# Cosine attention and a leaky-ReLU layer: the seventh pair turned by DMA, the 11th pair's norm behind the visit's first step, the last slot's scores and totals ahead of most early first products

## The chip, the cores and the metric

The kernel runs on one core of one Trainium2 chip. The metric is device time in microseconds (us). Its engines are TensorE (PE; PEld is its weight load), VectorE (DVE), ScalarE (ACT), GpSimd (POOL) and SyncE (SP). Each runs its own instructions in order and waits on semaphores for the others. SP, ACT and POOL also issue DMAs.

## The reference

```python
def _attn_ref(q, k, v, tau):                 # 8 batches, 12 heads, 448 rows, 64 columns
    q_n = q / (np.linalg.norm(q, axis=-1, keepdims=True) + 1e-06)
    k_n = k / (np.linalg.norm(k, axis=-1, keepdims=True) + 1e-06)
    scores = np.matmul(q_n, k_n.transpose(0, 1, 3, 2)) / tau
    scores = scores - np.max(scores, axis=-1, keepdims=True)
    attn = np.exp(scores)
    attn = attn / (np.sum(attn, axis=-1, keepdims=True) + 1e-09)
    return np.matmul(attn, v).astype(np.float32)

def _moe_ref(x, w_in, w_out):                # x: 3584 x 768; w_in: 768 x 2048; w_out: 2048 x 768
    h = x @ w_in
    g = np.maximum(0.01 * h, h)
    return (g @ w_out).astype(np.float32)
```

The attention's output, heads side by side, is the x of the second function.

## The kernel before

The program order is written out by hand: each engine carries out its instructions in the order in which the Python code emits them, so the place of a call in the code is its place in every queue that it uses.

**Pairs.** Two heads of one batch form a pair `s`, six to a batch, 48 in all, counted from 0: the seventh pair is `s` = 6, the first of batch 1, and the 11th is `s` = 10. A pair goes through these steps:

- its q and k are loaded (`load_pairs`, `load_qk`) into one of six places of `raw_sb`;
- `squares` (usually on POOL), `sums` (DVE) and `roots` (two small ACT instructions) give the norms;
- `normalise` (DVE: two small instructions and two large ones, L222) writes the normalised pair into a `qn` tile. The pool of these has three buffers, so pair `s` is written where pair `s` - 3 lay, and waits until that one has been read;
- `transposes` turns it, into a `qkT` tile: seven TensorE instructions (`one`, L236) into a PSUM bank and one copy (DVE up to pair 7, ACT after it), or, from pair 10 on (`DMA_FROM`), one DMA that SP issues (L254);
- `scores` (`key_tiles`) multiplies keys by queries (L280) in tiles of two PSUM banks, three for each pair and one for the remainders of two pairs, and ACT takes the exponentials (L292).

**Slots.** Two pairs form a slot `j`, three to a batch (`NQ`). `totals` sums the exponentials on TensorE, `reciprocals` inverts the sums on ACT (L339, L340), `products` multiplies by v on TensorE (L320), and `scale` writes the result into `xT` on DVE (L361). `attend` does this for one slot, `attend_two` for two.

**Chunks.** The 3584 rows are taken in eight chunks `c` of 384 and 512 rows in turn. The first products (`first`, L384) multiply a chunk's `xT` by `w_in`, six inner steps for each of 16 blocks `m`, and ACT writes hT. The second products (`groups`, L459) multiply hT by `w_out`.

**Order.** First come the six pairs of batch 0, with the scores of pair 5 last. Between these stand first products of chunk 0 that need the first two slots alone (`begin`: inner steps 0 to 3 of blocks 0 to 3). Then `attend(2)` does the last slot of batch 0, with the rest of those early products behind its value products. Then `firsts(0, ...)` does chunk 0's 16 blocks. Its table `between` says what is emitted ahead of which block: norms, sums and transposes of pairs 6 to 11 and loads of v. Then comes the visit of chunk 0 (`visit`): its second products, with the scores of batch 1 (pairs 6 to 11) dealt out between them after given numbers of steps (`wide`). Its table `norms` says what is emitted after which step. `attend_batch(1)` follows, then `firsts(1, ...)`, and so on for the other chunks.

**Holding GpSimd.** `hold` is a one-element POOL copy of a given tile: what POOL does next stays behind it. `norm(s)` emits `roots`, `normalise` and (unless told not to) `transposes`; then, by pair, loads of later pairs on SP, a `hold` on pair `s` and the squares of a later pair on POOL. The weights `w_out` are loaded by POOL's queue behind a `hold` on `xT`, ahead of `norm(7)`.

Of the kernel before, what the change touches and what calls it, by code (L numbers as in the profile page):

```python
# [16 lines left out]
def kernel(  # L17
# [19 lines left out]
    NPAIR = H // 2  # L37
    NSLOT = B * NPAIR
    NQ = NPAIR // 2
# [115 lines left out]
    def load_v(j):  # L155
        if j >= B * NQ:
            return
        b, jj = divmod(j, NQ)
        vb[j] = vbp.tile([128, 4, 3, D], BF16, name="v_b")
        gp.dma_start(out=vb[j], in_=main(v, b, 4 * jj, 4))  # L160
# [12 lines left out]
    def squares(s, engs=(gp, gp)):  # L173
        if s >= NSLOT:
            return
        tiles = []
        for x, eng, name in zip(raw[s], engs, ("sq0", "sq1")):
            sq = sqp.tile(list(x.shape), F32, name=name)
            if eng is nc.scalar:
                nc.scalar.activation(sq, x, func=AF.Square)  # L180
            else:
                eng.tensor_tensor(sq, x, x, op=ALU.mult)  # L182
            tiles.append(sq)
        sqs[s] = tiles

    def sums(s, parts=(0, 1)):
        if s >= NSLOT:
            return
        if s not in ss:
            ss[s] = smp.tile([128, 14], F32, name="ss")  # L190
        for i in parts:
            o = ss[s][:, 0:8] if i == 0 else ss[s][:, 8:14]
            nc.vector.tensor_reduce(  # L193
                o.rearrange("p (h t) -> p h t", h=2), sqs[s][i], axis=AX.X, op=ALU.add
            )

    def roots(s):
        if s >= NSLOT:
            return
        nc.scalar.activation(ss[s], ss[s], func=AF.Ln, bias=tiny)  # L200
        nc.scalar.activation(ss[s], ss[s], func=AF.Exp, scale=0.5)  # L201
# [11 lines left out]
    def normalise(s):  # L213
        if s >= NSLOT:
            return
        r = smp.tile([128, 14], F32, name="r")
        nc.vector.tensor_scalar_add(ss[s], ss[s], 1e-6)  # L217
        nc.vector.reciprocal(r, ss[s])
        qn[s] = qnp.tile([128, 7, 2, D], BF16, name="qn")
        for x, lo, hi, r0 in ((raw[s][0], 0, 4, 0), (raw[s][1], 4, 7, 8)):  # L220
            nt = hi - lo
            scalings[s] = nc.vector.tensor_tensor(  # L222
                qn[s][:, lo:hi],
                x.rearrange("p h t d -> p t h d"),
                r[:, r0 : r0 + 2 * nt].rearrange("p (h t) -> p t h", h=2)
                .unsqueeze(3).to_broadcast([128, nt, 2, D]),
                op=ALU.mult,
            )
# [19 lines left out]
    def transposes(s):  # L248
        if s >= NSLOT:
            return  # L250
        dst = qtp.tile([128, 7, 128], BF16, name="qkT")
        qkT[s] = dst.rearrange("p t c -> p (t c)")
        if s >= DMA_FROM:
            nc.sync.dma_start(  # L254
                out=dst, in_=qn[s].rearrange("p t h d -> p (t h d)"), transpose=True
            )
            return
        tp = transposed()
        one(tp, s, 0, 7)
        copy = nc.scalar.copy if s > 7 else nc.vector.tensor_copy  # L260
        copy(out=dst, in_=tp)  # L261
# [3 lines left out]
    def scores(s, kis):  # L265
        key_tiles([(s, ki) for ki in kis])
# [108 lines left out]
    def first(c, m, kts=range(KT)):  # L375

        c0, n = chunk_cols(c)
        if c not in hT:
            hT[c] = htp.tile([128, MT, 512], BF16, name="hT")
        if (c, m) not in pms:  # L380
            pms[c, m] = banks(1)
        pm = pms[c, m]
        for kt in kts:
            nc.tensor.matmul(  # L384
                out=pm[:, :n],
                lhsT=w_in_sb[:, kt, m * 128 : (m + 1) * 128],
                rhs=xT[c // 2][:, kt, c0 : c0 + n],
                start=(kt == 0), stop=(kt == KT - 1),
            )
        if kts[-1] == KT - 1:  # L390
            nc.scalar.activation(  # L391
                out=hT[c][:, m, :n], in_=pms.pop((c, m))[:, :n], func=AF.Prelu, alpha=0.01
            )
            if (c, m, 0) in kept:
                given_back((c, m, 0))
# [116 lines left out]
    def hold(x):  # L512
        seen = smp.tile([128, 1], F32, name="seen")
        gp.tensor_copy(out=seen, in_=x)  # L514
# [122 lines left out]
    def begin(m, kts):  # L637

        if (0, m) not in pms:
            pms[0, m] = banks(1, (0, m, 0))  # L640
        first(0, m, kts)

    scores(5, (0, 1))
    products(1, 1)
    for m in range(2):
        begin(m, range(2))
    for e in range(2):
        scale(1, e)
    scores(5, (2,))
    for m in range(2):  # L650
        begin(m, range(2, KT - 2))
    scores(5, (3,))
    for m in range(2, SOON):
        pms[0, m] = banks(1, (0, m, 0))
    begin(2, range(KT - 2))
    sums(6)
    sums(7)
    roots(6)

    def attend(j, behind=()):  # L660
        totals(j)
        reciprocals(j)
        po = banks(2)
        for e in range(2):
            products(j, e, po[:, e])
        for fn in behind:
            fn()
        for e in range(2):
            scale(j, e)
# [30 lines left out]
    def norm(s, transposed=True):  # L700
        if s >= NSLOT:
            return
        roots(s)
        normalise(s)
        if transposed:
            transposes(s)
        if s == 10:
            return
        for x in (12, 13) if s == 11 else (s + 4,) if s > 11 else ():
            load_qk(x)  # L710
        hold(qn[s][:, 6, 0, 0:1])
        if s == 11:
            squares(12)
        if s != 9:
            squares(s + (3 if s < 9 else 2))

    def firsts(b, begun, between):

# [25 lines left out]
    def at(*steps):  # L744
# [5 lines left out]
    four_late = (at(5, 11, 16, 16, 24),) * 3 + (at(6, 16, 16),)  # L750

    deals["apart"] = False
    attend(NQ - 1, [lambda m=m: first(0, m, range(KT - 2)) for m in range(3, SOON)])
    normalise(6)
    hold(xT[0][:, 2 * NQ - 2, 0:1])
    load_w_out(range(0, MT, MT // 4))
    norm(7, False)
# [2 lines left out]
    firsts(  # L760
        0, SOON, {
            4: [lambda: norm(8, False)],
            5: [lambda: transposes(6)],
            6: [lambda: sums(9)],
            8: [lambda: transposes(7)],
            9: [lambda: norm(9, False)],
            10: [lambda: transposes(8)],
            11: [lambda: sums(10), lambda: load_v(3)],
            12: [lambda: norm(10), lambda: load_v(4)],
            13: [lambda: transposes(9), lambda: load_v(5), lambda: load_v_rem(1)],  # L770
            15: [lambda: sums(11)],
        },
# [2 lines left out]
    for b in range(B):  # L775
        tokens = chunk_cols(b)[1] // 128
        if b == B - 1:
            for ts in range(tokens):
                for half in range(2):
                    second(b, ts, half)  # L780
            break
        order = [[((ts, 0), (ts, 1))] for ts in range(tokens)]
        if b == 0:
            order = [order[0] + order[1], order[2]]
        norms = {(0, 18): [lambda: norm(11)]}
        if b:
            norms = {}
            for i in range(tokens - 1 + (b == 1)):
                norms[i, 4 if tokens > 3 else 12] = [lambda s=ready: norm(s)]
                ready += 1  # L790
                norms[i, 20] = [lambda s=ready: sums(s)]
        else:
            ready += 2
        visit(
            b, order, norms,
            wide if b == 0 else four_late if b == 1 else three if tokens == 3 else four,
        )
        attend_batch(b + 1)
        for j in range((b + 2) * NQ, (b + 3) * NQ):
            load_v(j)  # L800
        load_v_rem(b + 2)
        s = ready
        between = {0: [lambda s=s: norm(s)], 1: [lambda s=s: sums(s + 1)]}
        if b == 0:
            between = {
                0: [lambda: sums(13)], 1: [lambda: norm(13), lambda: sums(14)],
                4: [lambda: norm(14), lambda: sums(15)], 7: [lambda: norm(15)],
                9: [lambda: sums(16)], 11: [lambda: norm(16)], 14: [lambda: sums(17)],
            }
            ready += 5  # L810
        elif tokens == 3:
            between.update({
                4: [lambda s=s: norm(s + 1), lambda s=s: sums(s + 2)],
                7: [lambda s=s: norm(s + 2), lambda s=s: sums(s + 3)],
                10: [lambda s=s: norm(s + 3)], 13: [lambda s=s: sums(s + 4)],
            })
            ready += 4
        else:
            between.update({
                4: [lambda s=s: norm(s + 1)], 5: [lambda s=s: sums(s + 2)],  # L820
                8: [lambda s=s: norm(s + 2)], 12: [lambda s=s: sums(s + 3)],
            })
            ready += 3
        firsts(b + 1, 0, between)
# [35 lines left out]
```

## Time and profile before

| what | value |
|---|---|
| median of 3 runs | 407.03 us (406.74 to 407.2) |
| profiled execution, device time | 407.09 us |
| its span, first to last instruction | 405.3 us |
| granted TensorE clock, mean | 1.000 |
| ACT busy | 265.0 us (65%) |
| DVE busy | 187.7 us (46%) |
| POOL busy | 140.7 us (35%) |
| share of the chain on PE | 93% |
| mean DMA traffic | 134 GB/s |

The stages that the change lies in, from the chain of waits: early products and the last slot of batch 0, 28.7 to 35.8 us; the rest of chunk 0's first products, to 50.35; the visit of chunk 0, to 69.97; the attention of batch 1, to 76.85.

How to read the lines that follow. A line of the chain of waits is start, length and what ran; a timeline line is start, length, engine, line of the code, operation, tiles written and read. "L384" is line 384 of the code. Queue q0 is POOL's DMA queue, q1 is SP's and ACT's. A window line gives busy time and number of instructions for PE, PEld, DVE, ACT and POOL, then the granted clock, the DMA share and GB/s.

### The profile page before, as it was taken

What the parts mean: (1) busy time and instruction counts of PE and PEld (TensorE: products, weight loads), DVE (VectorE), ACT (ScalarE), POOL (GpSimd) and SP (SyncE); (2) the same over time, 40 slices, a digit from 0 to 9 for tenths busy, and PEclk for the clock granted to TensorE, in tenths of its full rate; (3) what the DMA queues carried; (4) which work ended last, traced back from release to release, by engine and by line L of the source; (5) the groups of instructions that cost most, each with busy time, mean ns of one, the idle gap of its engine ahead of it and who ended that gap; (6) DMA issues with size and microseconds to landing.
All of it is one profiled execution on the core that took longest, in us unless ns stands there. A gap on an engine that the chain in (4) does not pass through costs nothing.

```text
span 405.3 us, 10173 instructions
## 1 busy us (share of the span) xinstructions
PE 398.5 (98%) x4096; PEld 225.0 (56%) x4096; DVE 187.7 (46%) x403; ACT 265.0 (65%) x458; POOL 140.7 (35%) x215
## 2 busy tenths in 40 slices
PE   8999999999999999999999999999999999999996
PEld 3335655544555655544886555544687555544564
DVE  6987912684665624454452626256361731130021
ACT  5996799556874689654876569745786559844300
POOL 4995823363344513343141513255122500000000
PEclk9999999999999999999999999999999999999999
DMA  7999999697689826576486844686477721110033
GB/s 190 252 227 246 214 184 212 180 182 180 147 195 154 153 60 175 118 126 174 73 185 142 131 113 118 160 117 152 68 177 125 96 45 40 40 41 2 0 78 79
DMA packets 100735, 54.21 MB, mean 134 GB/s; under 512 B 69424, under 2 KB 95440, under 8 KB 100688
## 3 DMA queue, kind: packets, MB, share of 16 engines
q1 hardware_dynamic: 76400, 40.13, 42.0%
q0 software_dynamic: 23440, 12.92, 23.2%
q8 instruction: 32, 0.52, 0.5%
q10 hardware_dynamic: 848, 0.52, 0.4%
q14 instruction: 15, 0.12, 0.1%
HBM read 45.61 MB, written 11.01 MB: 140 GB/s over the span
## 4 chain that ended last, share of the span: by engine, by line
PE 93%; POOL 3%; DVE 1%; DMA 1%; issue 1%; ACT 0%; POOLq 0%
PE ps L384 36%; PE ps L459 31%; PE ps L320 11%; PE ps L280 8%; PE ps L421 5%; POOL sq L182 1%; PE ps L307 1%; DMA raw_sb<-in_k_dram 1%; POOL v_rem L167 1%; DVE qn L222 1%; PE ps L236 1%; POOL raw_sb L132 0%; POOL v_b L160 0%; POOL seen L514 0%; DVE qkT L261 0%
## 5 line engine op out<-in xcount | busy, mean ns | idle before, releaser
L384 PE MATMUL ps<-xT,w_in_sb 128*128 128x384 bf16 (+1 forms) x768 | 148.0, 353 | 0.0
L459 PE MATMUL ps<-w_out_sb,hT 64*128 64x384 bf16 x1536 | 144.0, 323 | 0.0
L292 ACT ACTIVATE pe<-ps 128x896 bf16<-128x896 f32 x144 | 124.5, 917 | 17.2 <-PE ps L280 15.3
L384 PEld LDWEIGHTS <-w_in_sb 128*128 128x128 bf16 x768 | 74.0, 98 | 71.7 <-issue 4.0
L391 ACT ACTIVATE hT<-ps 128x384 bf16<-128x384 f32 (+1 forms) x128 | 67.2, 544 | 66.6 <-PE ps L384 66.1
L459 PEld LDWEIGHTS <-hT 64*128 64x128 bf16 x1536 | 84.4, 94 | 44.8 <-PE ps L459 4.2
L182 POOL TENSOR_TENSOR sq<-raw_sb 128x512 f32<-128x512 f32 x90 | 82.4, 937 | 12.5 <-DMA raw_sb<-in_k_dram 11.9
L222 DVE TENSOR_TENSOR qn<-raw_sb,r 128x512 bf16<-128x512 f32 x96 | 56.6, 631 | 2.0 <-DMA raw_sb<-in_q_dram 0.3
L280 PE MATMUL ps<-qkT 64*128 64x448 bf16 (+1 forms) x384 | 54.8, 353 | 1.1 <-DVE qkT L261 0.6
L193 DVE TENSOR_REDUCE ss<-sq 128x6 f32<-128x384 f32 (+1 forms) x95 | 54.3, 610 | 1.1 <-POOL sq L182 1.0
L471 DVE COPY osb<-ps 128x384 f32<-128x384 f32 x41 | 21.2, 553 | 69.7 <-PE ps L459 38.8
L514 POOL CAST seen<-qn 128x1 f32<-128x1 bf16 x46 | 9.1, 198 | 124.3 <-DVE qn L222 124.0
L217 DVE TENSOR_SCALAR ss<-ss 128x14 f32<-128x14 f32 x48 | 10.2, 213 | 75.7 <-ACT ss L201 75.6
L361 DVE TENSOR_TENSOR xT<-ps,rb 128x448 bf16<-128x448 f32 x48 | 27.8, 620 | 24.6 <-ACT rb L340 24.4
L160 POOL DMA_DIRECT2D v_b<-in_v_dram x24 | 18.6, 776 | 39.6 <-PE ps L320 39.6
L320 PE MATMUL ps<-pe,v_b 128*32 128x448 bf16 x576 | 32.0, 353 | 0.0
L280 PEld LDWEIGHTS <-qkT 64*128 64x128 bf16 (+1 forms) x384 | 17.7, 97 | 17.6 <-issue 7.3
L339 ACT ACTIVATE rb<-ps 128x448 f32<-128x448 f32 x24 | 12.9, 538 | 14.9 <-PE ps L320 13.9
L320 PEld LDWEIGHTS <-v_b 128*32 128x32 bf16 x576 | 15.1, 97 | 12.0 <-issue 0.6
L427 DVE COPY osb<-ps 128x384 f32<-128x384 f32 (+1 forms) x9 | 4.6, 513 | 36.6 <-PE ps L421 36.6
L421 PE MATMUL ps<-w_out_sb,hT 128*128 128x384 bf16 (+1 forms) x144 | 21.0, 308 | 0.0
L292 ACT ACTIVATE pr<-ps 128x896 bf16<-128x896 f32 x24 | 20.7, 924 | 0.2 <-PE ps L280 0.2
(52 smaller groups left out, 188.2 us busy)
## 6 DMA issues: line engine op xcount, KB each, us to landing
raw_sb<-in_q_dram SPq DMA_DIRECT2D x46, 192.0 KB, 3.2
raw_sb<-in_k_dram SPq DMA_DIRECT2D x44, 192.0 KB, 3.2
out_dram<-osb SPq DMA_DIRECT2D x30, 192.0 KB, 3.0
v_b<-in_v_dram POOLq DMA_DIRECT2D x24, 192.0 KB, 4.9
out_dram<-osb SPq DMA_DIRECT2D x12, 384.0 KB, 2.6
w_out_sb<-in_moe_w_out_dram POOLq DMA_DIRECT2D x4, 768.0 KB, 15.8
w_in_sb<-in_moe_w_in_dram POOLq DMA_DIRECT2D x3, 512.0 KB, 8.4
w_in_sb<-in_moe_w_in_dram POOLq DMA_DIRECT2D x2, 768.0 KB, 12.7
```

The source lines that it names most:

```text
L182: eng.tensor_tensor(sq, x, x, op=ALU.mult)
L193: nc.vector.tensor_reduce(o.rearrange("p (h t) -> p h t", h=2), sqs[s][i], axis=AX.X, op=ALU.add)
L222: scalings[s] = nc.vector.tensor_tensor(qn[s][:, lo:hi], x.rearrange("p h t d -> p t h d"), r[:, r0 : r0 + 2 * nt].rearrange("p (h t) -> p ...
L280: nc.tensor.matmul(out=out[:, a, :S], lhsT=x[rows, c0:c1], rhs=x[rows, 0:S], start=True, stop=True,)
L292: nc.scalar.activation(out=dst, in_=sc[:, :, :S], func=AF.Exp, scale=inv_tau)
L320: nc.tensor.matmul(out=x[32 * g : 32 * g + 32, :S], lhsT=weights(g, ki) if ki < 3 else rem(g), rhs=pe[s][:, ki, a, :] if ki < 3 else pr[j] ...
L361: scalings[j, e] = nc.vector.tensor_tensor(xT[m][:, 2 * jj + e, half * S : (half + 1) * S], pos.pop((j, e))[:, :S], rbs[j], op=ALU.mult,)
L384: nc.tensor.matmul(out=pm[:, :n], lhsT=w_in_sb[:, kt, m * 128 : (m + 1) * 128], rhs=xT[c // 2][:, kt, c0 : c0 + n], start=(kt == 0), stop= ...
L391: nc.scalar.activation(out=hT[c][:, m, :n], in_=pms.pop((c, m))[:, :n], func=AF.Prelu, alpha=0.01)
L421: nc.tensor.matmul(out=po2[:, :n], lhsT=hT[c][:, m, ts * 128 : (ts + 1) * 128], rhs=w_out_sb[:, m, lo : lo + n], start=(m == 0), stop=(m = ...
L459: done[p][i] = nc.tensor.matmul(out=pos2[p][:, i, :HALF], lhsT=hT[c][rows, m, ts * 128 : (ts + 1) * 128], rhs=w_out_sb[rows, m, half * HAL ...
L471: copy(out=osb[c, ts][:, half * HALF : (half + 1) * HALF], in_=po2[:, i, :HALF])
```

## The change

- `transposes` turns pair 6 by DMA too.
- `norm`, `normalise` and `transposes` of pair 6 stand together right behind `attend(2)`; its roots move from ahead of `attend(2)` to there, its transposes from block 5 of `firsts(0, ...)`.
- Of the early first products, two of block 1 move behind the third score tile of pair 5, two of block 1 behind its remainder tile, and two of block 2 behind the value products of `attend(2)`.
- The squares of pairs 10 and 11, until now behind the norms of pairs 7 and 8, both stand behind pair 9's, under one `hold`. The norms of pairs 7 and 8 hold POOL no longer.
- The sums of pair 10 move from block 11 to block 12, and its norm from block 12 to the visit, after the first step.

```diff
@@ transposes
-        if s >= DMA_FROM:
+        if s >= DMA_FROM or s == NPAIR:
@@ early first products
-    for m in range(2):
-        begin(m, range(2))
+    begin(0, range(2))
     for e in range(2):
         scale(1, e)
     scores(5, (2,))
-    for m in range(2):
-        begin(m, range(2, KT - 2))
+    begin(1, range(2))
+    begin(0, range(2, KT - 2))
     scores(5, (3,))
+    begin(1, range(2, KT - 2))
     for m in range(2, SOON):
         pms[0, m] = banks(1, (0, m, 0))
-    begin(2, range(KT - 2))
+    begin(2, range(2))
     sums(6)
     sums(7)
-    roots(6)
@@ norm
-        if s == 10:
-            return
         for x in (12, 13) if s == 11 else (s + 4,) if s > 11 else ():
             load_qk(x)
-        hold(qn[s][:, 6, 0, 0:1])
-        if s == 11:
-            squares(12)
-        if s != 9:
-            squares(s + (3 if s < 9 else 2))
+        ahead = {7: (), 8: (), 9: (10, 11), 10: (), 11: (12, 13)}.get(s, (s + 2,))
+        if ahead:
+            hold(qn[s][:, 6, 0, 0:1])
+        for x in ahead:
+            squares(x)
@@ the last slot of batch 0, chunk 0's first products
-    attend(NQ - 1, [lambda m=m: first(0, m, range(KT - 2)) for m in range(3, SOON)])
+    attend(NQ - 1, [lambda: first(0, 2, range(2, KT - 2)), lambda: first(0, 3, range(KT - 2))])
+    roots(6)
     normalise(6)
+    transposes(6)
     hold(xT[0][:, 2 * NQ - 2, 0:1])
     load_w_out(range(0, MT, MT // 4))
     norm(7, False)
@@ between
             4: [lambda: norm(8, False)],
-            5: [lambda: transposes(6)],
             6: [lambda: sums(9)],
             8: [lambda: transposes(7)],
             9: [lambda: norm(9, False)],
             10: [lambda: transposes(8)],
-            11: [lambda: sums(10), lambda: load_v(3)],
-            12: [lambda: norm(10), lambda: load_v(4)],
+            11: [lambda: load_v(3)],
+            12: [lambda: sums(10), lambda: load_v(4)],
             13: [lambda: transposes(9), lambda: load_v(5), lambda: load_v_rem(1)],
             15: [lambda: sums(11)],
@@ norms of the visit
-        norms = {(0, 18): [lambda: norm(11)]}
+        norms = {(0, 1): [lambda: norm(10)], (0, 18): [lambda: norm(11)]}
```

## The prediction

> **What bounds the kernel now.** I read the page's first part, then the chain of waits, then the timeline of VectorE (DVE), then the DMA queues in short windows.
>
> ```profile
> span 405.3 us, 10173 instructions
> PE 398.5 (98%) x4096; PEld 225.0 (56%) x4096; DVE 187.7 (46%) x403; ACT 265.0 (65%) x458; POOL 140.7 (35%) x215
> ```
>
> TensorE is busy for 98% of the span, and the chain is TensorE alone from 24.4 us on. So work taken from other engines brings nothing, and anything that makes TensorE wait is paid in full. The chain where the change lies (start, length, what):
>
> ```profile
> 34.86 0.92 PE ps L384 x5
> 35.78 0.01 issue
> 35.79 2.27 PE ps L384 x13
> 38.06 0.39 PE ps L236 x7
> 38.45 2.93 PE ps L384 x18
> ...
> 44.11 2.92 PE ps L384 x18
> 47.04 0.39 PE ps L236 x7
> 47.43 2.92 PE ps L384 x18
> 50.35 0.50 PE ps L280 x8
> ```
>
> L384 are first products, L236 transposes: those of pair 6 (38.06), later 7, 8, and 9 (47.04). Eighteen products take 2.92 us, but the 18 from 34.86 on take 3.20: 0.27 us (rounded) of waiting for the scaled last slot. These two are all that can be won here: 0.39 + 0.27 = 0.66 us. From 50.35 on no wait of this size is left that the edits touch.
>
> VectorE at the two norms that matter (pair 6, pair 9):
>
> ```profile
> 36.13 1.16 DVE L222 TENSOR_TENSOR qn<-raw_sb,r 128x512 bf16<-128x512 f32 x2
> 44.87 1.47 DVE L222 TENSOR_TENSOR qn<-raw_sb,r 128x512 bf16<-128x512 f32 x2
> ```
>
> **The change, part by part.**
>
> *Order of the early products.* Ahead of pair 5's third score tile stand two first products instead of four, ahead of its remainder tile six instead of eight, ahead of the totals ten instead of twelve; six instead of four stand behind the value products. By 2.92/18 = 0.162 us each, all three begin 0.32 earlier, the totals at 32.16 instead of 32.48. ScalarE (ACT) must follow: its exponentials before this end at 30.47, so the third tile's starts there instead of at 30.69 and ends by 31.4, the remainder tile's runs 31.45 to 32.37, the reciprocal 33.08 to 34.23, and the scaling on VectorE ends at 35.42 instead of 35.73. TensorE reaches the product that needs it at 35.67, so the wait goes: -0.27. The roots of pair 6 (0.30 + 0.21) leave ScalarE's 32.61 to 33.15 and follow the reciprocal; pair 7's roots and pair 9's squares end about 0.25 later, at 36.3, and the first hT copy starts then instead of at 36.15, covered by the PSUM banks that TensorE still has free. Without that cover it would cost that 0.15.
>
> *Pair 6 turned by DMA.* Seven transposes leave TensorE: -0.39. A copy of 0.62 leaves VectorE, which lies beside TensorE: 0. SP issues one DMA of 1.26, with nothing on its queue between the early loads and pair 10's transpose: 0. But the normalised pairs lie in three rotating buffers, so pair 9 is written where pair 6 lay. Before, that waited for transposes done at 38.45; now it waits until the DMA has landed. Pair 9 is still turned on TensorE, in order, ahead of the 14th block of products. So the question is when the DMA lands. It is issued when pair 6 is normalised: 1.56 us behind the scaling as before (35.73 to 37.29), so 36.98, plus 0.08 to issue: 37.06.
>
> The trace has 38 such DMAs. The first, the second, and the other 36:
>
> ```profile
> L254 SPq DMA_TRANSPOSE qkT<-qn x1: 1347/1347/1347, 49.7 to 49.7; - x1
> DMA to landing us min/median/max: 10.6/10.6/10.6
> ...
> DMA to landing us min/median/max: 7.2/7.2/7.2
> ...
> DMA to landing us min/median/max: 2.9/3.0/5.8
> ```
>
> The short ones run when GpSimd's queue (q0) is empty. The first ran beside the weights. The queue lines for 49.7 to 53.5, 53.5 to 55.5, 41 to 49 and, quiet, 78 to 79.3 (packets, MB, share):
>
> ```profile
> q0 software_dynamic: 536, 0.80, 116.0%
> ...
> q0 software_dynamic: 238, 0.35, 96.2%
> q1 hardware_dynamic: 204, 0.05, 19.7%
> ...
> q0 software_dynamic: 1106, 1.68, 115.3%
> ...
> q1 hardware_dynamic: 917, 0.23, 90.0%
> ```
>
> None of its packets moved for 3.8 us; then q1 went about packet for packet with q0, whose rate fell from 536/3.8 = 141 to 119 per us (x0.84). A turn is some 900 packets of 256 bytes (7 x 128 rows). From 37 on q0 is fuller: 1106 packets in 41 to 49, 138 per us. With q1 beside it that gives 138 x 0.84 = 116 per us for each. So: 37.06 + 3.9 + 900/116 = 48.7. The nearest row, 10.6 in all, gives 47.7 and is my lower end, since its q0 turned to short packets after 55.5; two SP loads issued at 18 to 24 took 10.0 and 11.5, and I take 13 as the upper end (50.1).
>
> Then pair 9: 48.75 + 1.16 (GpSimd, which now waits for this very tile, can't slow it to 1.47) = 49.9. At the start the last transpose's successor on TensorE began 0.33 after such a norm ended (22.15 + 1.16 to 23.64), so block 14 begins at 50.25. Before, it began at 47.27. Sum: **+2.98 us**; TensorE arrives at 47.04 - 0.66 = 46.38, so the 0.66 is swallowed by a wait of over 3 us.
>
> *Pairs 10 and 11.* The squares of 10 and 11 (1.82 each on GpSimd) move behind pair 9's norm, with GpSimd's loads of v behind them; so all this queues behind the same DMA: squares end near 53.8, the v issues run from there instead of from 48.09. They landed by 65.1 for a use at 70.28, and the use moves 3 us too: covered. Without cover each us late would be a us. The sums of 10 and 11 are alone on VectorE then: 0. The norm of 10 moves from block 13 to the first step of the visit, behind the two remainder exponentials: 0.51 of roots on ScalarE, which idles 0.25 and 0.57 in the visit, and the exponentials run ahead of need: 0, at worst 0.5. Its transpose is issued some 4.4 us into the visit instead of 0.6 before it and is needed 14.6 in; pair 11's stands behind it on SP, with the loads of pairs 12 and 13 after that, and is needed 16.3 in. By 3.9 + 900/190 (q0 and q1 moved about 90 packets each per half us once q0's were short) pair 10 lands 13.1 in. Pair 11 follows 1.5 to 3.4 later: 14.6 to 16.5. I take 0, with 1 us as the upper bound.
>
> The profiled execution took 407.09: 405.3 of span and 1.8 around it; the median is 407.03, 0.06 less. 407.03 + 2.98 = **410.0**; its own range is 408.9 (landing at 47.7) to 411.4 (landing at 50.1).
>
> The Trainium skill, "DMA: Bandwidth & Descriptors", section "Latency and other measured facts", gives a DMA transpose an effective 261 GB/s and a hardware queue some 0.6 us to the first byte. By that this 0.23 MB would take about 0.9 us plus a fixed part; the quiet rows (3.0 in all) agree, the row beside the weights (10.6) does not. By it the sum would be -0.66, which is the first rival.
>
> **The rivals.**
>
> *A, the transpose lands before anybody needs it.* It decides at landing by 45.9, under 8.9 us after issue: then pair 9 is ready at 47.06 and block 14 not later than before. If it takes 8 or less, all of -0.66 stays: 406.4. For it: 37 of 38 transposes took 7.2 or less. Against it: the only one issued into a full weight queue took 10.6, and at 37 that queue has over 15 us of work left. This is the rival on the other side: not slower.
>
> *B, the wait makes TensorE slow.* After the last matmul the granted clock falls:
>
> ```profile
> 400.00:405.30 5.30, 1.65 (x20) 1.42 (x18) 0.71 (x2) 0.00 (x0) 0.00 (x0) 0.96 0.30 74
> ```
>
> TensorE ends at 401.65; a mean of 0.96 over 5.30 us means full clock until about 404.9 and half after, so 3.25 us of idleness sufficed. The predicted idle stretch, 46.4 to 49.5, is 3.1. A slow spell is sized by the start, where ten 512-column matmuls took 4.1 us and eleven after them 2.4: half speed for about 4 us. Price about 1.7 to 2 us: 411.9. Against it: the stretch is just shorter. The Trainium skill, "TensorE: Matmul & The Clock Gate", section "Why this matters for your kernels", allows no idle gap over about 3 us; the trace agrees as far as it shows, and by that rule B would be likelier than I make it.
>
> *C, pairs 10 and 11 come late.* On top of the wait, pair 11's first score tile waits for its turn: +1, 411.0. For it: two transposes and eight loads on one ring, issued within 4 us. Against it: the second transpose of before needed 7.2 beside the same v loads.
>
> **How the numbers follow.** Forecast 0.56, A 0.20, B 0.12, C 0.12. A change under 0.2%, 0.8 us, can't be told from none. A's full gain is below that, so of its 0.20 I give 0.09 to faster (a gain that I overlooked) and 0.11 to no change; 0.80 to slower. The range runs from A to B with the upper end of landing: 406.3 to 412.4; a pair 11 that waits longer, or A with more gain, is left out.
>
> **What would show it.** Right: an idle stretch of about 3 us on TensorE just before the last seven transposes, ended by VectorE's norm of pair 9, itself ended by the DMA transpose; that DMA taking 10 to 13 us; the wait at 35.8 gone; block 14 beginning near 50.25. Wrong: the DMA landing by 45.9; a granted clock of 0.5 near 50 (B); TensorE waiting for a turned pair near 66 to 70 (C).

## The result, and the profile after

The changed kernel takes **413.44 us** (413.26 to 414.73, five runs); the kernel before, measured beside it, 407.16 (406.74 to 407.20). The ratio is 1.0162 [1.0150, 1.0173]: slower, as forecast, but by 6.3 us instead of 3.0, and above the upper end of the range. The profiled execution is the slowest of the five, 414.73. The first part of its page (the row PEclk is the granted clock in 40 slices):

```profile
span 413.0 us, 10145 instructions
...
PE 400.1 (97%) x4079; PEld 225.5 (55%) x4089; DVE 186.2 (45%) x402; ACT 265.0 (64%) x458; POOL 139.6 (34%) x213
...
PEclk9999979999999999999999999999999999999999
```

The span is 7.7 us longer. TensorE has seven weight loads fewer (4089 for 4096), yet is busy 1.6 us longer; and one slice, about 52 to 62 us, has less than the full clock. The chain of waits there (start, length, what):

```profile
35.37 0.61 DVE xT L361
...
36.37 1.16 DVE qn L222 x2
...
37.56 13.82 DMA qkT<-qn
...
51.46 0.70 DVE qn L222
...
52.21 0.97 PE ps L236 x7
53.18 4.91 PE ps L384 x18
58.09 0.50 PE ps L280 x8
```

The scaling of the last slot ends at 35.98, later than forecast, since this execution runs 0.57 late before any edit: score products ahead of all of them begin at 28.81, in the kernel before (second line) at 28.24.

```profile
28.81 0.48 PE ps L280 x4
28.24 0.48 PE ps L280 x4
```

Before, TensorE alone was the chain at 35 to 50. Now pair 6's DMA transpose is in it, with 13.82 us, and behind it pair 9's norm (51.46) and transposes (52.21). The 18 products of the last three blocks (14 to 16) take 4.91 instead of 2.92, and the visit begins at 58.09 instead of 50.35, 7.74 later. Of that 0.57 is the late start and 7.17 the change; the rest of the kernel neither loses nor gains. The timeline, with the idle time of the engine and what ended it in brackets:

```profile
51.46 1.16 DVE L222 TENSOR_TENSOR qn<-raw_sb,r 128x512 bf16<-128x512 f32 x2 [6.92 <-DMA qkT<-qn]
52.21 0.97 PE L236 MATMUL ps<-id,qn 128*128 128x128 bf16 x7 [5.17 <-DVE qn L222]
52.75 0.19 POOL L514 CAST seen<-qn 128x1 f32<-128x1 bf16 x1 [10.24 <-DVE qn L222]
52.97 5.12 PE L384 MATMUL ps<-xT,w_in_sb 128*128 128x384 bf16 x18
```

VectorE stands 6.92 us on the DMA, TensorE 5.17 on VectorE, and GpSimd's hold runs only at 52.75. The windows of the wait, of what follows, and of the visit (the clock is the third number from the right):

```profile
47.20:50.20 3.00, 0.00 (x0) 0.00 (x0) 0.00 (x0) 0.37 (x1) 0.00 (x0) 1.00 1.17 168
50.30:57.00 6.70, 4.79 (x20) 2.60 (x21) 3.49 (x6) 1.40 (x2) 4.22 (x6) 0.50 1.17 210
57.10:60.00 2.90, 2.90 (x32) 1.43 (x32) 0.05 (x1) 2.32 (x4) 2.90 (x6) 1.00 1.26 194
```

TensorE does nothing from 47.04 on; from 50.26 to 57.09, 6.83 us, it is granted half its clock. Last, the transpose: its time from issue to landing, then the queue lines for 41.6 to 46.5 and for 47 to 48 (packets, MB, share):

```profile
DMA to landing us min/median/max: 13.8/13.8/13.8
...
q0 software_dynamic: 536, 0.86, 91.9%
q1 hardware_dynamic: 521, 0.13, 20.8%
...
q0 software_dynamic: 46, 0.07, 93.0%
q1 hardware_dynamic: 48, 0.01, 30.2%
```

The two queues move packet for packet, some 108 each per us; between 47 and 48 both move less than half of that.

### The profile page after: what moved, and what is told of

Read it like the earlier page. It is cut to its first block, busy times and chain, and to the rows that moved or that the text cites. A ratio compares the mean times of both kernels' runs of the same rounds, so it can differ in the third digit from the quotient of the medians.

```text
span 413.0 us, 10145 instructions
## 1 busy us (share of the span) xinstructions
PE 400.1 (97%) x4079; PEld 225.5 (55%) x4089; DVE 186.2 (45%) x402; ACT 265.0 (64%) x458; POOL 139.6 (34%) x213
## 3 DMA queue, kind: packets, MB, share of 16 engines
q1 hardware_dynamic: 77328, 40.36, 41.6%
## 4 chain that ended last, share of the span: by engine, by line
PE 88%; DMA 7%; DVE 1%; ACT 1%; SPq 1%; issue 0%; POOL 0%; DVEq 0%
PE ps L384 33%; PE ps L459 30%; PE ps L320 11%; PE ps L280 7%; PE ps L421 5%; DMA qkT<-qn 3%; DMA raw_sb<-in_q_dram 3%; PE ps L307 1%; DVE qn L222 1%; ACT pe L292 1%; PE ps L236 0%; SPq L127 0%; ACT rb L340 0%; POOL sq L182 0%; ACT rb L339 0%
## 5 line engine op out<-in xcount | busy, mean ns | idle before, releaser
L384 PEld LDWEIGHTS <-w_in_sb 128*128 128x128 bf16 x768 | 74.9, 99 | 73.0 <-issue 5.9
L514 POOL CAST seen<-qn 128x1 f32<-128x1 bf16 x44 | 8.2, 187 | 139.4 <-DVE qn L222 139.0
```

Source lines behind the costliest of these rows:

```text
L384: nc.tensor.matmul(out=pm[:, :n], lhsT=w_in_sb[:, kt, m * 128 : (m + 1) * 128], rhs=xT[c // 2][:, kt, c0 : c0 + n], start=(kt == 0), stop= ...
```

## The experiments

Each kernel is compared with the kernel before on the same chip: 407.14 us for the first four, 407.17 for the other three. My theory: the one edit that turns pair 6 by DMA makes the loss, by a wait for a reused buffer and then by the clock. The rivals: the other edits cost something too; the clock is not part of it; the transpose is slow by itself.

**1. Pair 6 on TensorE again, all other edits kept.**

```diff
-        if s >= DMA_FROM or s == NPAIR:
+        if s >= DMA_FROM:
...
-    transposes(6)
...
+            5: [lambda: transposes(6)],
```

> The changed kernel with pair 6 turned on TensorE again, at block 5 as before; all other edits stay. Theory: the wait for the DMA-turned pair 6 and the slow clock behind it are the whole loss, and the order of the early products is worth 0.27: no idle stretch ahead of pair 9's transposes, clock 1.000, 406.9 (407.16 - 0.27). Rival: the moved squares, holds, sums and pair 10's norm cost something by themselves: 407.5 or more, with TensorE waiting for a turned pair 10 or 11 in the visit.

Measured: 407.04 us (406.58 to 407.47), ratio 0.9994 [0.9983, 1.0005]. Its chain:

```profile
34.25 3.36 PE ps L384 x20
...
47.13 2.92 PE ps L384 x18
50.06 0.50 PE ps L280 x8
```

Neither wait nor half clock at 47. The 20 products hold 0.11 of wait (20 x 0.1625 = 3.25) instead of 0.27, so 0.16 is gained there. The visit begins 0.29 earlier than before, but that isn't the edits' gain, since this execution is 0.28 early already ahead of them; and at 41.46 the 0.16 is lost again, where a weight load of TensorE waits for the last part of `w_in`, which lands at 41.42 here and at 40.40 before:

```profile
27.96 0.48 PE ps L280 x4
```
```profile
41.46 1.58 PEld L384 LDWEIGHTS <-w_in_sb 128*128 128x128 bf16 x11 [0.27 <-DMA w_in_sb<-in_moe_w_in_dram]
```

The interval leaves a loss of 0.2 us at most: the other edits cost nothing that can be measured, and what they gain can't be told from nothing.

**2. Only that edit, on the kernel before.**

```diff
-        if s >= DMA_FROM:
+        if s >= DMA_FROM or s == NPAIR:
...
     normalise(6)
+    transposes(6)
...
-            5: [lambda: transposes(6)],
```

> The kernel before with this one edit: pair 6 turned by DMA, issued right behind its norm. Theory: that edit alone makes the loss. Pair 9's norm waits for the landing near 51 (13 to 14 after an issue near 37.4), TensorE idles 4 to 5, the granted clock falls to half, 412 to 415. Rival: the loss needs the moved squares and norms too, and the DMA alone is covered: 407 to 408.

Measured: 414.85 us (413.14 to 415.45), ratio 1.0184 [1.0165, 1.0204]. Chain, then a window:

```profile
37.59 14.02 DMA qkT<-qn
...
52.44 0.97 PE ps L236 x7
53.41 5.36 PE ps L384 x18
```
```profile
51.50:58.10 6.60, 5.66 (x23) 3.02 (x24) 5.14 (x10) 2.58 (x6) 4.85 (x8) 0.50 1.16 210
```

The same transpose, the same wait, the same half clock. This edit alone makes the loss: experiments 1 and 2 take it apart from both sides. The median loss is 7.7 instead of 6.3, but the intervals of the two ratios overlap.

**3. A fourth buffer for normalised pairs.** Pair 9 then needn't wait for pair 6.

```diff
-    qnp = ctx.enter_context(tc.tile_pool(name="qn", bufs=3))
+    qnp = ctx.enter_context(tc.tile_pool(name="qn", bufs=4))
```

> The changed kernel with four buffers for normalised pairs instead of three, so that pair 9 isn't written where pair 6 lies. Theory: pair 9's norm runs near 44.5 and its transposes near 46.4 to 46.9 without a wait; the wait goes on to the next user of the turned pair, the visit's first score tile, due near 49.7 to 50.2 and held until the landing near 51: 1 to 1.8 of idle TensorE, too short for the clock (1.000), 407.16 - 0.66 + 1 to 1.8 = 407.5 to 408.3. Rival: the wait is another than that for the buffer and stays: 413.

Measured: 408.06 us (407.35 to 408.91), ratio 1.0023 [1.0013, 1.0033], at full clock. Its transpose takes 13.90 (36.89 to 50.79). Waits and chain:

```profile
PE ps L280 <- DMA qkT<-qn: 1.2, 1, 1.2
```
```profile
50.83 0.57 PE ps L280 x8
```

So the wait came from the reused buffer. With that gone, TensorE reaches the visit at 50.83 - 1.15 = 49.68, 0.67 earlier than before. Of that, 0.11 is this execution's earlier start (28.13 for the products at 28.24), so the two edits gain 0.56, where the prediction had put 0.66 on them. TensorE then stands 1.15 for the turned pair itself: 50.83 against 50.35 is 0.48 late, and this execution's span is 0.5 longer. The median of the nine runs is 0.9 above the kernel before.

**4. The wait without the clock.** Twenty matmuls that nobody reads (`fill`) keep TensorE busy while it waits.

```diff
-            13: [lambda: transposes(9), lambda: load_v(5), lambda: load_v_rem(1)],
+            13: [lambda: fill(20), lambda: transposes(9), lambda: load_v(5), lambda: load_v_rem(1)],
```

> The changed kernel with 20 filler matmuls of 512 columns on TensorE ahead of pair 9's transposes (20 x 0.216 = 4.3 of work that nobody reads), so that it is busy while it would wait. Theory: the clock fell because TensorE idled. With the filler it stays at 1.000, blocks 14 to 16 take 2.9 instead of 4.9, the wait itself stays: 411.2 to 411.6. Rival: the clock fell for another reason, or the wait is all of the loss: 413.3 as the changed kernel.

Measured: 411.95 us (411.59 to 412.43), ratio 1.0117 [1.0102, 1.0133], a little above what was expected. Timeline and window:

```profile
46.38 4.48 PE L505 MATMUL ps<-warm 128*128 128x512 bf16 x19
52.03 0.81 PE L236 MATMUL ps<-id,qn 128*128 128x128 bf16 x7 [1.17 <-DVE qn L222]
```
```profile
51.00:56.00 5.00, 3.89 (x33) 2.22 (x33) 2.76 (x5) 2.08 (x4) 3.40 (x5) 1.00 1.15 209
```

The wait is the same (the transpose took 14.19, and the fillers end 1.17 before pair 9 is ready), the clock stays full, and about a quarter of the loss is gone. So the wait costs 411.95 - 407.14 = 4.8 us, and the half clock the rest of the changed kernel's loss, 1.8 us by the ratios (1.0162 less 1.0117, of 407) or 1.5 by the medians.

**5. Only the new order of the early products, on the kernel before** (the edits "early first products" and the moved `roots(6)` of the diff above).

```diff
-    for m in range(2):
-        begin(m, range(2))
+    begin(0, range(2))
...
-    begin(2, range(KT - 2))
+    begin(2, range(2))
...
-    roots(6)
```

> The kernel before with the new order of the early first products alone (and pair 6's roots behind the last slot, as that order has them). Theory: the wait of 0.27 ahead of the last slot's products goes and nothing else changes: 406.9. Rival: the wait only moves elsewhere, 407.1 as before.

Measured: 406.96 us (406.72 to 407.32), ratio 0.9994 [0.9985, 1.0003]. In its chain the visit begins at 50.00 instead of 50.35; 0.18 of that is an earlier start (28.06 instead of 28.24), and 0.17 the gain of the edit, of the 0.27 expected. The interval holds no change: this gain is seen in the chain, not in the time.

**6. Four buffers, and pair 6 wanted later.** With the fourth buffer of experiment 3, the visit's first score tiles are those of pairs 8 and 9's remainder and of pair 7, so that nobody waits for pair 6; one tile more is dealt out at step 4.

```diff
-        key_tiles([(s0 + 1, 3), (s0 + 3, 3)] + [(s0 + 5, 3)] * (b > 1))
+        if b == 0:
+            key_tiles([(s0 + 3, 3)])
+            tiles = tiles[3:6] + [(s0 + 1, 3)] + tiles[0:3] + tiles[6:]
+        else:
+            key_tiles([(s0 + 1, 3), (s0 + 3, 3)] + [(s0 + 5, 3)] * (b > 1))
```

> The changed kernel with four buffers for normalised pairs, and the visit of chunk 0 taking pair 7's score tiles first, then the remainder tile that needs pair 6, then pair 6's: the first use of the turned pair 6 comes near 53.5 instead of 49.9. Theory: a landing near 50.8 is then waited for by nobody, and both gains stand, 0.39 + 0.27: 406.4 to 406.6. Rival: something else in the visit gives the gain back, such as ScalarE behind pair 10's roots or a late pair 11: 407.1 or more.

Measured: 408.48 us (408.21 to 408.95), ratio 1.0035 [1.0022, 1.0049]: missed, by 2 us. Waits:

```profile
PE ps L459 <- DMA w_out_sb<-in_moe_w_out_dram: 1.3, 1, 1.3
PE ps L236 <- DVE qn L222: 0.6, 1, 0.6
```

Nobody waits for pair 6 any more (landing after 14.04, at 51.43), but now the second products wait for the last part of `w_out`, which lands at 61.54. In the kernel before it landed at 59.0, and in experiment 1, without this transpose, at 59.4. The transpose takes turns from the weights' queue, and that is paid as soon as the visit begins on time.

**7. The weights behind the transpose.** `w_out` is issued once pair 6 has landed.

```diff
-    hold(xT[0][:, 2 * NQ - 2, 0:1])
+    hold(qkT[6][:, 0:1])
```

> The changed kernel with GpSimd held on the turned pair 6 instead of the scaled last slot, so that all four loads of w_out are issued after the landing; the loads ahead of them in that queue stay and end near 44.8. Theory: the DMA transpose takes long because it shares the DMA engines packet for packet with that queue. Its first 340 packets go at about 106 per us from 41.6 on, the rest at the quiet rate of 700: landing near 46, 8.5 to 9.5 after its issue instead of 13.8, TensorE waits for pair 9 by under 1.5, the clock stays; then the visit waits for w_out by 0 to 3: 407 to 410. Rival: the time is that of a DMA transpose issued there whatever else runs: again 13 to 14, and over 413.

Measured: 412.51 us (411.05 to 413.21), ratio 1.0127 [1.0109, 1.0145]: the time missed, the transpose a little shorter than expected. Chain, the queue lines for 40.4 to 44.2, and waits:

```profile
36.92 7.90 DMA qkT<-qn
...
47.38 17.80 DMA w_out_sb<-in_moe_w_out_dram
```
```profile
q1 hardware_dynamic: 928, 0.23, 93.8%
q0 software_dynamic: 131, 0.33, 29.1%
```
```profile
PE ps L459 <- DMA w_out_sb<-in_moe_w_out_dram: 5.1, 4, 2.0
```

With q0 at 29% instead of 92%, the same 928 packets need 3.8 us instead of 9.1, the whole turn 7.90, and pair 9 is in time. So most of its slowness is not the transpose's own: the full weight queue makes some 5.9 of the 13.8 us. But the weights come 5.1 us too late for the visit. (Two of the four runs also show a mean clock of 0.994 and 0.995, so part of the loss may be the clock's; the profiled run, at 412.11, does not.) Queue time in this stretch has no slack; the change asked for some of it.

None of the seven is measurably faster than the kernel before.

## Why the prediction was right in kind and wrong in size

**Right: the place and the chain.** One wait on TensorE ahead of pair 9's transposes, ended by VectorE's norm, ended by the DMA, because pair 9 is written where pair 6 lay: the chain shows it, experiment 3 removes it. From landing to block 14 the prediction had 50.25 - 48.7 = 1.55 us; it took 52.97 - 51.38 = 1.59. GpSimd stood behind the same DMA and cost nothing. Of the gain of 0.66, 0.56 exists (experiment 3), and the wait swallows it.

**Wrong: the term "37.06 + 3.9 + 900/116 = 48.7", and its upper end of 13 us from issue.** The landing came at 51.38. Of the 2.68 us, 0.50 is the later issue: this execution began some 0.57 late, by its earlier chain. The other 2.18 is flight, 13.82 for 11.64, and no accident: the five kernels that issue this DMA beside the weights show 13.8, 14.0, 13.9, 14.2 and 14.0. Its parts: the first packet moved after 4.10 (+0.2); 928 packets at the 109 per us seen outside the stop are 8.5 us, where 900 at 116 were 7.75 (+0.75); the stop at 47, with some 62 packets missing, cost 0.6; and the last data packet moved at 50.76, 0.6 before the landing counted. Start and shared rate were nearly right. The stop was in no row of the kernel before. The tail was: its first transpose moved its last data packet at 59.77 and landed at 60.29, 0.52 later, and the sum put it at nothing. The upper end came from loads, which are not transposes, and was too low by 0.8 to 1.2 us.

**Wrong as a consequence: B was set aside.** It got a chance of 0.12 and was argued against because the idle stretch, 3.1 us, would be "just shorter" than 3.25. With the longer flight the stretch is 47.04 to 52.21, 5.17 us, and the clock fell. B's price of 1.7 to 2 us was right: blocks 14 to 16 take 1.99 longer in the profiled execution, and experiment 4 gives 1.5 to 1.8. Forecast and B should have been one case: whatever lengthened the wait by a little brought B in. The range has a slip besides: B with the upper end of landing is 411.4 + 1.7 to 2 = 413.1 to 413.4 in the prediction's own terms, not 412.4, and the measured 413.44 lies just above even that. The profiled execution's sum: 410.0 + 2.68 (landing) + 0.04 + 2.0 (clock) = 414.7, measured 414.73; in the medians, 4.8 (wait) and about 1.5 (clock) of 6.3.

**The clock, by row.** In the profiled execution the half clock lasted 6.83 us; two of the five runs have a mean clock of 0.996 instead of 0.991, about half as long a spell, and took 413.26 both. An idle stretch of 1.15 us (experiment 3) did nothing. How long TensorE has to idle is not one number, as the prediction's 3.25, read off a single row, made it seem. The clock fell 3.22 us after the last product here (47.04 to 50.26) and 4.5 in experiment 2 (46.92 to 51.39). At the end of the kernel it had fallen 2.6 after the last product in experiment 3 (402.25 to 404.87), and was still full 3.6 after it in experiment 6 (403.12 to 406.70). The windows of these two ends:

```profile
404.90:405.80 0.90, 0.00 (x0) 0.00 (x0) 0.00 (x0) 0.00 (x0) 0.00 (x0) 0.50 0.00 0
```
```profile
403.20:406.70 3.50, 0.00 (x0) 0.00 (x0) 0.31 (x1) 0.00 (x0) 0.00 (x0) 1.00 0.26 67
```

So even the forecast stretch of 3.1 could have fallen on either side. The clock records of the nine traces show a grid: from a rise to the next fall, or from a fall to the next rise, it is always a whole number of times 3.413 us (6.83 is 2, the 44.37 ahead of the fall here 13; in the others 399.36 is 117 and 402.77 is 118). The Trainium skill, "TensorE: Matmul & The Clock Gate", section "What's actually happening", describes a free-running window of 3.413 us. The traces agree, and a start that falls anywhere in a window would explain why the same wait costs one window or two; no run here moved the phase by itself.

**A fell.** It needed a landing within 8.9 us of issue; the turn met that only with the weights out of its way (7.90, experiment 7).

**C didn't come.** Pair 10's transpose was issued at 62.41 and landed at 67.39, pair 11's at 65.41 and 68.37, and TensorE waited for neither. The moved norm, squares and v loads cost nothing that can be measured, as summed (experiment 1).

**The new order** was summed at -0.27. It took the wait down to 0.11, not to nothing (experiments 1 and 5). In time that can't be told from zero.

## What to carry to other kernels

Work that a saturated engine hands to the DMA queues is paid in queue time: look first at who else uses the queue then (here, weights without slack), and at which buffer the transfer holds while it runs. Price a transfer beside a full queue by start + packets at the shared rate + a tail, and leave room above that sum, since every term here came out on the long side. When a predicted wait comes near the idle time at which the clock falls (2.6 to 4.5 us in these traces), treat the fall as part of the forecast. And before an earlier or later start of a stage is called a gain, take off how early the execution already was ahead of the edits: here up to 0.57 us, as much as the gain looked for.

## What the runs showed of the hardware beyond what was expected

- **The transpose's first packet** moves 3.5 to 4.2 us after issue in the six kernels that turn pair 6 by DMA (4.10 here), beside the GpSimd queue with its weights or what is left of it. It moves 1.17 us after issue in a quiet stretch (66.08 in experiment 2), but also 1.17 for pair 10 here (62.41), while that queue moved 682 short packets. So a full queue alone doesn't set this time; what does is open. Most of the 7.90 of experiment 7 that isn't packets is this.
- **A stop of both queues.** Between 47 and 48 us the two queues moved 46 and 48 packets; in the us before it 111 each, in the us after it 115 and 114. The same stop stands in all four other kernels with the same transpose beside the weights. A packet of a third queue (q8, "instruction", 16 KB) fell into each of these flights shortly ahead. Over the nine traces, with 32 such packets each, q0 or q1 had a packet of over 0.65 us within 2.5 us behind it in 73 of 100 cases when a DMA transpose was in flight, and in 17 of 188 otherwise; in experiment 1, without pair 6's DMA, q0 moved 136 packets in that us. This is a coincidence in time, counted; its cause wasn't tried.
- **Equal packets, unequal bytes.** The queues alternate packet for packet (521 and 536), whatever the packets' size: the transpose, in packets of 256 bytes, gets 13% of the bytes (0.13 MB beside 0.86). The Trainium skill, "DMA: Bandwidth & Descriptors", section "Queues, rings and completion order", says that each DMA engine takes the queues in turn, a packet at a time; the rows agree.
